# Making the normalised rows early, pairing the rows and summing in 32-column strips at the hand-over from the feed-forward block to the spectral block (backward pass, one core)

## Chip, cores, metric

One core of one Trainium2 chip. The metric is the device time of one execution in microseconds (us). The engines are TensorE (PE in the profile; PEld is its weight load), VectorE (DVE), ScalarE (ACT), GpSimd (POOL) and SyncE (SP).

A ratio below is the mean time of one kernel's fast runs over the mean of the kernel before's fast runs of the same rounds, with a 95% interval. It is therefore not quite the ratio of the medians that are quoted beside it.

## The reference

A block with two branches, forward and backward, in bf16. Cut to what matters:

```python
def _A_ref(x, w_r, w_i):                       # spectral branch
    X = rfft2(x.astype(float32)); X = X * (w_r + 1j * w_i)
    return irfft2(X, s=(S, D)).astype(bfloat16)
def _B_ref(x, w_gate, w_up, w_down):           # gated feed-forward
    g = x @ w_gate; u = x @ w_up
    return (g * u) @ w_down
mod = silu(c) @ w_mod                          # sa, ca, ga, sb, cb, gb: six rows of 576
h = layernorm(x) * (1 + ca) + sa
x1 = x + ga * _A_ref(h)
h = layernorm(x1) * (1 + cb) + sb
out = x1 + gb * _B_ref(h)
# returned: out and the gradients of x, w_r, w_i, w_gate, w_up, w_down, c, w_mod
```

S = 2048 rows, D = 576, F = 4608. The kernel holds the rows as 16 tiles of 128 rows; "a row" below is such a tile, 128 x 576, and j counts them. n is the normalised x1, y the output of the spectral branch, b the gradient that reaches the second layernorm's output, and gx the gradient of x1.

Three sums over all 2048 rows are wanted for the gradients of the modulation: the sum of b (for sb), of b * n (for cb) and of gx * y (for ga).

## The kernel before

The feed-forward backward is a loop of 18 steps (about 300 to 1186 us). Then comes the hand-over, to which the change belongs. For each row it

- finishes b with the last four products of the loop (`gh2_last`), whose result shrinks to bf16 in the first half of the row's fp32 accumulator. The freed second half (`acc_h`) then takes the row x1 that is loaded,
- normalises x1 on ScalarE, goes backward through the layernorm on VectorE and ScalarE, and stores gx,
- forms the three sums on TensorE, and
- begins the spectral backward (`fold`, then `stage_a`).

Remaining matmuls of the loop's weight gradients ("filler") are mixed in, so that TensorE has work while rows are prepared. Their results leave PSUM through VectorE (`gwd_halves`) or ScalarE (`gw_block`), and their banks come from the same ring as those of `gh2_last` and `stage_a`. Cut:

```python
def gh2_last(j):
    for h in range(2):
        b = sbk()                                          # next bank of the ring
        gh2_mms(NP - 1, j, h, bank[:, b, 0:288])
        tt(acc_b(j)[:, hs], acc[:, j, hs], bank[:, b, 0:288], ADD)      # VectorE

def diag_sums(a, b, j, b0, b1, c1, col):                   # sum of a*b on the diagonal of a^T b
    for m, (d0, n) in enumerate(CH):                       # chunks 128,128,128,128,64
        if col is not None:
            mm(bank[0:n, b1, col + m:col + m + 1], a[:, d0:d0 + n], ones[:, 0:1], ...)
        mm(..., a[:, d0:d0 + n], b[:, d0:d0 + n], ...)     # 128x128, its diagonal is used

def load_n(j):
    nx[j] = nx_r.next() if j < 2 else acc_h(j)
    sp.dma_start(nx[j][:], x1_d[:, j, :])                  # SyncE's queue

def row_front(j):
    n = nx[j]
    act(n[:], n[:], ACT.Identity, bias=nmr2[:, j:j + 1], scale=rstd2[:, j:j + 1])
    ...ln_bwd_a: gn = b*(1+cb), sum of gn, t2 = gn*n, sum of t2
def row_back(j):
    ...ln_bwd_b: gx from gn, n and the two sums; gx stored; fold(gx*(ga))
def row_sums(j):
    diag_sums(acc_b(j), nx[j], j, 2, 3, 0, 192)
    diag_sums(st_a[j][0], yl[j], j, 5, 3, 64, None)        # gx and y

for j in range(18):                                        # cut
    want = min(16, 2 + 5 * j // 4)
    while done < want: gh2_last(done); done += 1; ...fill.run(1.0)
    while loaded < min(done, j + 3): load_n(loaded); loaded += 1
    if j < 16: row_front(j); row_back(j)
    if fill.left() > 12.0 or j > 15: fill.run(1.0 if j < 16 else 2.0)
    if 2 <= j: row_sums(j - 2)
    if fill.left() > 12.0 or j > 15: fill.run(1.0)
    if 2 <= j: row_a(j - 2)                                # stage_a
```

After the loop, stage B of the spectral backward begins with the rest of the filler. A further filler follows, the forward's down projection ("the first y matmul").

Of the kernel before, what the change touches and what calls it, by code (L numbers as in the profile page):

```python
# [81 lines left out]
def build(ctx, tc, A_x, A_w_r, A_w_i, B_w_gate, B_w_up, B_w_down, c_in, w_mod, grad_out,  # L82
# [8 lines left out]
    def dram(name, shape, dt=BF):  # L91
        return nc.dram_tensor(name, list(shape), dt).ap()
# [5 lines left out]
    x1_d = dram("x1_d", [128, 16, D])  # L98
    gx1_d = dram("gx1_d", [128, 16, D])
# [109 lines left out]
    with tc.manual_schedule(engines={PE}):  # L209
# [756 lines left out]

        po.memset(gbacc[:], 0.0)
        for p in range(NP):
            gu_block(p)
            if p + 1 < NP:  # L970
                load_wgu(p + 1)
                load_wT(p + 1)
            load_wd(p)
            if p == NP - 1:
                break
            if p:
                for _, f in grads(p - 1, dbank):
                    f()
            else:
                for k in range(3):  # L980
                    transposes(k)
            for j in range(16):
                gh2_block(p, j)
# [4 lines left out]
        nx_r = Ring(span(ST, 2, 1152), [D])  # L988
        yl_r = Ring(span(ST + 2304, 2, 1152) + span(ST, 2, 1152), [D])
        F_r = Ring(span(ST + 4608, 4, 1152), [D])  # L990
        tg_r = Ring(span(ST + 9216, 3, 1152), [D])
        gx_r = Ring(span(ST + 12672, 3, 1152), [D])
        t2_r = Ring(span(ST + 16128, 4, 1152), [D])
        s_r = Ring([8704, 8736, 8768, 9952], [8], FP32)
        sring = [0, 1, 4, 6, 7]
# [25 lines left out]
        def diag_sums(a, b, j, b0, b1, c1, col):  # L1021

            for m, (d0, n) in enumerate(CH):
                if col is not None:
                    mm(bank[0:n, b1, col + m:col + m + 1], a[:, d0:d0 + n], ones[:, 0:1], j == 0 and m == 0, False, skip_group_check=True)
                if m < 4:
                    mm(bank[:, b0, 128 * m:128 * m + 128], a[:, d0:d0 + n], b[:, d0:d0 + n], j == 0 and m == 0, False, skip_group_check=True)
                else:
                    mm(bank[0:64, b1, c1:c1 + 64], a[:, 512:576], b[:, 512:576], False, False, skip_group_check=True)

        def column_sums(srcs, b, j, w):

            for h in range(2):
                for i, a in enumerate(srcs):
                    mm(bank[w * i:w * i + w, b + h, 0:288], ones[:, 0:w], a[:, 288 * h:288 * h + 288], j == 0, j == 15, skip_group_check=True)

# [5 lines left out]

        def load_n(j):

            nx[j] = nx_r.next() if j < 2 else acc_h(j)
            sp.dma_start(nx[j][:], x1_d[:, j, :])
# [53 lines left out]
        def row_front(j):  # L1100
            n = nx[j]
            act(n[:], n[:], ACT.Identity, bias=nmr2[:, j:j + 1], scale=rstd2[:, j:j + 1])
            gn, t2, s = tg_r.next(), t2_r.next(), s_r.next()
            ln_bwd_a(acc_b(j), n, mod[:, SCB, :], gn, None, t2, s)
            st_a[j] = (gn, t2, s)

        def row_back(j):
            gn, t2, s = st_a[j]
            gx, Fj = gx_r.next(), F_r.next()
            ln_bwd_b(nx[j], gn, t2, rstd2[:, j:j + 1], go[:, j, :], gx, s)  # L1110
            po.dma_start(gx1_d[:, j, :], gx[:])
            tt(gn[:], gx[:], mod[:, SGA, :], MUL)
            fold(Fj.unsqueeze(1), gn.unsqueeze(1), 1)
            st_a[j] = (gx, Fj)

        def row_sums(j):
            diag_sums(acc_b(j), nx[j], j, 2, 3, 0, 192)
            diag_sums(st_a[j][0], yl[j], j, 5, 3, 64, None)

        def row_a(j):  # L1120
            b = sbk()
            stage_a(st_a[j][1], b)
            evac_a(ac, b, j)
            if j % 2:
                b = sbk()
                for i in range(2):
                    stage_a_rem(st_a[j - 1 + i][1], b, i)
                evac_rem(ac, b, j - 1, 2)

        for j in range(2):  # L1130
            load_n(j)
            load1(yl, yl_r, y_d, j, sp)
        load_wdr(0, 9)
        done, loaded = 0, 2
        for j in range(18):
            want = min(16, 2 + 5 * j // 4)
# [5 lines left out]
            while loaded < min(done, j + 3):  # L1142
                load_n(loaded)
                loaded += 1
            if j < 16:
                row_front(j)
                row_back(j)
            if fill.left() > 12.0 or j > 15:
                fill.run(1.0 if j < 16 else 2.0)
            if 2 <= j < 18:  # L1150
                row_sums(j - 2)
            if fill.left() > 12.0 or j > 15:
                fill.run(1.0)
            if 2 <= j < 18:
                row_a(j - 2)
            if j < 14:
                load1(yl, yl_r, y_d, j + 2, sp)
# [4 lines left out]
            if j == 12:  # L1162
                load_wdr(9, 28)
                sp.dma_start(TI.rearrange("p a b c -> p (a b c)"), tabs["TI"][:, :])
                sp.dma_start(TBI.rearrange("p a b -> p (a b)"), tabs["TBI"][:, :])
            if j == 15:
                for t in W_r.t:
                    po.memset(t[:, :, :, DF:FP], 0.0)
                for u in range(2):
                    Ws[u] = W_r.next()  # L1170
                    load_W(Ws[u], u)
        sring = [4, 5]
# [14 lines left out]
        mk_r = Ring(span(ST + 16128, 2, 1152) + span(ST + 4608, 2, 1152), [D])  # L1187
# [9 lines left out]
        def diag_mask(b0, c1):  # L1197
            mk = mk_r.next()
            po.memset(mk[64:128, 512:576], 0.0)
            tt(mk[:, 0:512].rearrange("p (m d) -> p m d", m=4), bank[:, b0, :].rearrange("p (m d) -> p m d", m=4), ident.unsqueeze(1).to_broadcast([128, 4, 128]), MUL)  # L1200
            tt(mk[0:64, 512:576], bank[0:64, 3, c1:c1 + 64], ident[0:64, 0:64], MUL)
            return mk

        def col_mask(col):
            mk, cc = mk_r.next(), s_r.next()
            po.memset(mk[64:128, 512:576], 0.0)
            ve.tensor_copy(cc[:, 0:5], bank[:, 3, col:col + 5])
            for m, (d0, n) in enumerate(CH):
                ts(mk[0:n, d0:d0 + n], ident[0:n, 0:n], cc[0:n, m:m + 1], None, MUL)
            return mk  # L1210

        m_sga, m_scb, m_ssb, gbh = diag_mask(5, 64), diag_mask(2, 0), col_mask(192), mk_r.next()
        ve.tensor_copy(gbh[:], gbacc[:])

        def spread(rows, hi, lo):
            for h in range(2):
                for q0, src in ((0, hi), (64, lo)):
                    mm(bank[q0:q0 + 64, 6 + h, 0:288], ones[:, 0:64], src[:, 288 * h:288 * h + 288], True, True)
            ac.copy(halves(rows), bank[:, 6:8, 0:288])
# [55 lines left out]
        for s in range(9):  # L1275
# [3 lines left out]
            if s < 8:  # L1279
# [4 lines left out]
                if s == 0:  # L1284
                    spread(rows23, m_sga, m_ssb)
                fill.run(1.2)
                if s == 0:
                    spread(rows45, m_scb, gbh)
# [188 lines left out]
```

## Time and profile before

| | us |
|---|---|
| median of 15 runs | 1507.25 (1504.47 to 1509.69) |
| profiled execution | 1506.7 |
| loop, 350 to 1150 us: TensorE busy | 800.0 of 800 |
| hand-over, 1185.86 to 1285.40: TensorE busy | 87.4 of 99.5 |
| stage B up to the first y matmul | 9.3 |
| the rest | 212.0 |

The head of the page:

```profile
span 1506.7 us, 28428 instructions
...
PE 1467.3 (97%) x11221; PEld 981.1 (65%) x11244; DVE 779.9 (52%) x1734; ACT 548.5 (36%) x1048; POOL 345.8 (23%) x504
```

The table of stretches of the kernel before. Its columns are the stretch, its length, then busy time and instruction count per engine, the granted TensorE clock, the DMA share and GB/s. The second row is the hand-over, the third stage B.

```profile
core 0: us, PE busy (x) PEld busy (x) DVE busy (x) ACT busy (x) POOL busy (x), PEclk, DMA share, GB/s
350.00:1150.00 800.00, 800.00 (x6203) 562.09 (x6201) 340.63 (x620) 176.56 (x358) 164.00 (x226) 1.00 0.62 137
1185.86:1285.40 99.54, 87.41 (x873) 68.93 (x872) 72.13 (x208) 62.09 (x134) 26.13 (x41) 0.95 0.85 231
1285.40:1294.67 9.27, 9.27 (x83) 6.42 (x81) 2.19 (x3) 3.98 (x8) 0.33 (x3) 1.00 0.88 254
1294.67:1506.70 212.03, 200.46 (x1664) 144.47 (x1661) 150.28 (x341) 106.48 (x233) 54.81 (x86) 0.98 0.72 194
```

TensorE is full in the loop, where nothing is to be had, and loses time in the hand-over. The list of waits of the hand-over (who waited for whom, us in total, how often, the longest) says for what:

```profile
ACT arena L1102 <- DMA arena<-x_d: 14.0, 3, 6.3
DVE arena L1006 <- ACT arena L1102: 13.5, 5, 6.4
...
PE bank L943 <- ACT arena L889: 6.1, 2, 5.0
```

L1102 is the normalisation, and it waits for the load of x1. SyncE's queue in order of time shows the load (x_d) behind two transposing transfers, which hold the queue for 6.74 us together:

```profile
1222.57 6.74 SPq L830 DMA_TRANSPOSE arena<-arena  x2
1229.41 0.59 SPq L1046 DMA_DIRECT2D arena<-x_d  x1
1230.09 0.40 SPq L1050 DMA_DIRECT2D arena<-y_d  x1
```

The stop that follows can be traced through ScalarE, VectorE and TensorE in the timeline. The bracket is the idle time before an instruction, with what ended it.

```profile
1234.70 0.87 ACT L1102 ACTIVATE arena<-arena 128x576 bf16<-128x576 bf16 x1 [6.30 <-DMA arena<-x_d]
...
1235.60 0.46 DVE L1006 TENSOR_TENSOR arena<-arena 128x576 bf16<-128x576 bf16 x1 [6.43 <-ACT arena L1102]
...
1237.97 0.40 PE L943 MATMUL bank<-arena 128*128 128x288 bf16 x1 [4.95 <-ACT arena L889]
...
1238.16 0.44 PE L944 MATMUL bank<-arena 128*128 128x288 bf16 x1
...
1238.40 0.44 PE L945 MATMUL bank<-arena 128*128 128x288 bf16 x1
```

TensorE stood for 4.95 us. After that its 288-column matmuls start every 0.24 us instead of every 0.122 us. The Trainium skill says so of an array that has been idle for a while ("TensorE: Matmul & The Clock Gate", part 1). The stops of the hand-over add up to 12.1 us, and slow matmuls cost about 4 us more.

The sums of one row in TensorE's timeline take 1.07 us, from the start at 1208.51 to 1209.58:

```profile
1207.63 1.04 PE L888 MATMUL bank<-arena 128*128 128x256 bf16 x8
1208.51 0.17 PE L1025 MATMUL bank<-arena 128*128 128x1 bf16 x1
1208.53 0.22 PE L1027 MATMUL bank<-arena 128*128 128x128 bf16 x1
...
1209.43 0.22 PE L1029 MATMUL bank<-arena 128*64 128x64 bf16 x1
1209.58 1.05 PE L884 MATMUL bank<-arena 128*128 128x256 bf16 x8
```

### The profile page before, as it was taken

Reading aid. Unit: us, or ns where it says so; the run is one execution under the profiler, and the core shown is the slowest. Engines: PE = TensorE matmul, PEld = TensorE weight load, DVE = VectorE, ACT = ScalarE, POOL = GpSimd, SP = SyncE. Lnnn points to the kernel's source line nnn. Section 1 sums busy time; section 2 is a strip of 40 time slices with the busy share of each in tenths; the row PEclk is TensorE's granted clock in tenths of the full one; section 3 lists DMA queues with packets and bytes.
Section 4 is the critical chain, followed back from the end, with each engine's and each line's share of the span. In section 5 each row is a group of like instructions: output and inputs, shape, how many; then the busy total and the mean of one; then the engine's idle time right before and its main releaser. Section 6 shows DMA issues by size and latency. Waiting matters only on the chain.

```text
span 1506.7 us, 28428 instructions
## 1 busy us (share of the span) xinstructions
PE 1467.3 (97%) x11221; PEld 981.1 (65%) x11244; DVE 779.9 (52%) x1734; ACT 548.5 (36%) x1048; POOL 345.8 (23%) x504
## 2 busy tenths in 40 slices
PE   8999999999999999999999999999999988999998
PEld 5444444677667667667667668668668566776666
DVE  6533596543543443443453453453353776577766
ACT  6756675212221221221221221221221575333565
POOL 1344322203202202202202202202201113232211
PEclk9999999999999999999999999999999999999999
DMA  9656987958558548548548557557557469788873
GB/s 340 179 149 157 234 232 177 207 116 192 113 104 190 126 93 188 133 94 181 134 91 183 133 110 164 133 114 160 135 110 148 121 176 289 202 215 207 249 225 98
DMA packets 428762, 248.67 MB, mean 165 GB/s; under 512 B 319154, under 2 KB 403060, under 8 KB 428116
## 3 DMA queue, kind: packets, MB, share of 16 engines
q1 hardware_dynamic: 400418, 162.40, 48.6%
q0 software_dynamic: 27440, 83.65, 18.2%
q8 instruction: 88, 1.44, 0.4%
q10 hardware_dynamic: 770, 0.80, 0.2%
q14 instruction: 46, 0.38, 0.1%
HBM read 96.46 MB, written 74.20 MB: 113 GB/s over the span
## 4 chain that ended last, share of the span: by engine, by line
PE 84%; ACT 4%; DMA 4%; DVE 4%; issue 3%; POOL 1%; SPq 1%; DVEq 0%; POOLq 0%; ACTq 0%
PE bank L806 9%; PE bank L837 8%; PE bank L808 8%; PE bank L884 8%; PE bank L888 8%; PE bank L1082 6%; PE bank L943 5%; PE bank L946 4%; PE bank L945 4%; PE bank L944 4%; PE bank L370 3%; PE bank L801 3%; PE bank L374 3%; PE bank L904 2%; DMA arena<-in_w_mod_dram 1%
## 5 line engine op out<-in xcount | busy, mean ns | idle before, releaser
L957 DVE TENSOR_TENSOR arena<-arena,bank 128x576 f32<-128x576 f32 x256 | 193.1, 754 | 305.1 <-PE bank L946 305.1
L812 ACT CAST arena<-bank 128x512 bf16<-128x512 f32 x144 | 84.4, 586 | 384.6 <-PE bank L802 375.8
L943 PE MATMUL bank<-arena 128*128 128x288 bf16 x576 | 164.3, 285 | 6.3 <-ACT arena L889 6.1
L946 PE MATMUL bank<-arena 128*128 128x288 bf16 x576 | 164.9, 286 | 0.0
L945 PE MATMUL bank<-arena 128*128 128x288 bf16 x576 | 164.7, 286 | 0.0
L944 PE MATMUL bank<-arena 128*128 128x288 bf16 x576 | 164.4, 285 | 0.0
L884 PE MATMUL bank<-arena 128*128 128x256 bf16 x1152 | 149.5, 273 | 0.6 <-ACT arena L889 0.6
L888 PE MATMUL bank<-arena 128*128 128x256 bf16 x1152 | 149.8, 273 | 0.0
L1082 PE MATMUL bank<-arena 128*128 128x288 bf16 x1152 | 149.3, 288 | 0.2 <-ACT arena L1085 0.2
L806 PE MATMUL bank<-arena 128*128 128x512 bf16 x576 | 149.1, 381 | 0.0
L808 PE MATMUL bank<-arena 128*128 128x512 bf16 x576 | 147.8, 379 | 0.0
L1082 PEld LDWEIGHTS <-arena 128*128 128x128 bf16 x1152 | 112.0, 98 | 32.1 <-issue 3.5
L837 PE MATMUL bank<-arena 128*128 128x288 bf16 x1024 | 128.1, 286 | 0.0
L884 PEld LDWEIGHTS <-arena 128*128 128x128 bf16 x1152 | 110.7, 98 | 17.3 <-issue 4.5
L888 PEld LDWEIGHTS <-arena 128*128 128x128 bf16 x1152 | 112.4, 98 | 13.9 <-issue 0.2
L889 ACT CAST arena<-bank 128x256 bf16<-128x256 f32 x144 | 53.6, 372 | 185.4 <-PE bank L888 185.3
L837 PEld LDWEIGHTS <-arena 128*128 128x128 bf16 x1024 | 100.2, 98 | 28.2
L816 DVE TENSOR_TENSOR arena<-arena 128x512 bf16<-128x512 bf16 x144 | 61.3, 425 | 103.6 <-ACT arena L812 99.7
L734 POOL DMA_DIRECT2D arena<-ghh_d x36 | 20.1, 559 | 398.3 <-DVE arena L815 364.1
L806 PEld LDWEIGHTS <-arena 128*128 128x128 bf16 x576 | 50.5, 98 | 78.7 <-issue 31.5
L808 PEld LDWEIGHTS <-arena 128*128 128x128 bf16 x576 | 56.4, 98 | 68.0 <-issue 0.2
L813 ACT CAST arena<-bank 128x512 bf16<-128x512 f32 x144 | 84.8, 589 | 23.1 <-PE bank L808 23.1
(261 smaller groups left out, 2357.7 us busy)
## 6 DMA issues: line engine op xcount, KB each, us to landing
ghh_d<-arena POOLq DMA_DIRECT2D x72, 256.0 KB, 3.9
arena<-ghh_d POOLq DMA_DIRECT2D x36, 512.0 KB, 6.0
hh_d<-arena SPq DMA_DIRECT2D x36, 512.0 KB
arena<-hh_d SPq DMA_DIRECT2D x16, 1152.0 KB
out_dram<-arena POOLq DMA_DIRECT2D x67, 144.0 KB, 4.7
out_dram<-arena POOLq DMA_DIRECT2D x36, 256.0 KB, 5.1
arena<-in_B_w_down_dram POOLq DMA_DIRECT2D x18, 288.0 KB, 4.4
arena<-in_B_w_gate_dram POOLq DMA_DIRECT2D x18, 256.0 KB, 3.5
```

The costliest lines, as they stand in the source:

```text
L806: mm(bank[:, bg, :], w[:, m, fs], h2T[:, js, m, :], odd == 0 and m == 0, odd == 1 and m == 3)
L808: mm(bank[:, bu, :], w[:, 4 + k, fs], h2T[:, js, m, :], odd == 0 and k == 0, odd == 1 and k == 3)
L813: ac.copy(u[:], bank[:, bu, :])
L837: mm(bank[:, b0 + h, 0:288], sf[:, 0, fb, j, :], go[:, j, 288 * h:288 * h + 288], j == 0, j == 15)
L884: mm(bank[:, st["b"], 0:256], h2p[:, j, 128 * m:128 * m + 128], sf[:, 1 + w, :, j, :], j == 0, False)
L888: mm(bank[:, st["b"], 0:256], h2p[:, j, 128 * m:128 * m + 128], sf[:, 1 + w, :, j, :], False, j == 15)
L943: mm(o, xT[:, 1, 0, cs], wT[p][:, 0, 0, hs], True, False)
L944: mm(o, xT[:, 2, 0, cs], wT[p][:, 0, 1, hs], False, False)
L945: mm(o, xT[:, 1, 1, cs], wT[p][:, 1, 0, hs], False, False)
L946: mm(o, xT[:, 2, 1, cs], wT[p][:, 1, 1, hs], False, True)
L957: tt(dst, dst, src, ADD)
L1082: mm(bank[:, yb, 0:288], hl[:, fb % 18, 128 * (j % 2):128 * (j % 2) + 128], wdr[:, fb, 288 * h:288 * h + 288], fb == 0, fb == 35)
```

## The change

Its intent has three parts. First, make the normalised rows n in the loop, where ScalarE has time, and load them through GpSimd's queue instead of SyncE's. Second, do the layernorm backward on pairs of rows, with fewer and wider VectorE instructions and the scaling moved to ScalarE. Third, replace the diagonal products by column sums of b, b*n and gx*y: the products are made on VectorE and summed on TensorE by matmuls with ones in strips of 32 columns. With that the last products run one row further ahead, PSUM bank 3 joins the ring, gx is stored through SyncE's queue instead of GpSimd's, y is loaded in pairs of rows, and the weight rows of the later filler load in a different order. Cut to its core:

```diff
+        def keep_n(j):                                    # once a step, in the loop
+            t = prod_r.next().bitcast(BF)[:, 0:D]
+            d = t if j < 14 else nrow[:, j - 14, :]
+            po.dma_start(t, x1_d[:, j, :])
+            act(d, t, ACT.Identity, bias=nmr2[:, j:j + 1], scale=rstd2[:, j:j + 1])
+            if j < 14:
+                sp.dma_start(n_d[:, j, :], d)
...
-        sring = [0, 1, 4, 6, 7]
+        sring = [0, 1, 3, 4, 6, 7]
...
-        def diag_sums(a, b, j, b0, b1, c1, col):          # cut
+        def quarter_sums(a, b, q, start, stop):
+            for h in range(2):
+                r = slice(32 * (q + h), 32 * (q + h) + 32)
+                mm(bank[r, b, 0:288], ones[:, 0:32], a[:, 288 * h:288 * h + 288], start, stop, ...)
...
         def load_n(j):
-            nx[j] = nx_r.next() if j < 2 else acc_h(j)
-            sp.dma_start(nx[j][:], x1_d[:, j, :])
+            if j < 14:
+                po.dma_start(acc_h(j), n_d[:, j, :])
...
+        def front(i):                                     # a pair of rows
+            tt(gn[:], b_pair(i), opc, MUL)
+            tt(q[:], b_pair(i), n, MUL)
+            tt(t2[:], q[:], opc, MUL)
+            for k in range(2):
+                act(gn[:, k, :], gn[:, k, :], ACT.Copy, scale=rstd2[...], accum_out=s[:, k, 0:1])
+                act(t2[:, k, :], t2[:, k, :], ACT.Copy, scale=nrs2[...], accum_out=s[:, k, 1:2])
+        def back(i):
+            ...gx, its store (SyncE), gx*(ga), fold
+            tt(t2[:], gx[:], yl[i][:], MUL)
+        def sums_1(j):
+            quarter_sums(acc_b(j), 2, 0, j == 0, j == 15)
+            quarter_sums(st_a[j // 2][2][:, j % 2, :], 2, 2, j == 0, j == 15)
+        def sums_2(i):
+            for k in range(2):
+                quarter_sums(st_a[i][1][:, k, :], 5, 2 * k, i == 0, i == 7)
...
-        for j in range(18):
-            want = min(16, 2 + 5 * j // 4)
+        for j in range(19):
+            want = min(16, 3 + 5 * j // 4)
...
-            while loaded < min(done, j + 3):
+            while loaded < min(done, j + 6):
```

More of the change, by code (lines that the diff above doesn't have):

```diff
@@ L98, in build @@
     x1_d = dram("x1_d", [128, 16, D])
+    n_d = dram("n_d", [128, 16, D])
     gx1_d = dram("gx1_d", [128, 16, D])
@@ L965, in gh2_last @@
                 tt(acc_b(j)[:, hs], acc[:, j, hs], bank[:, b, 0:288], ADD)
+        nrow = mod[:, SSA:SSB + 1:SSB - SSA, :]
+        def keep_n(j):
[5 more added lines that the diff above has]
+                sp.dma_start(n_d[:, j, :], d)
         po.memset(gbacc[:], 0.0)
@@ L976, in build @@
             if p:
-                for _, f in grads(p - 1, dbank):
+                for i, (_, f) in enumerate(grads(p - 1, dbank)):
                     f()
+                    if i == 7 and p > 1:
+                        keep_n(p - 2)
+                        if p == NP - 2:
+                            keep_n(p - 1)
             else:
@@ L987, in build @@
         pl = NP - 1
-        nx_r = Ring(span(ST, 2, 1152), [D])
-        yl_r = Ring(span(ST + 2304, 2, 1152) + span(ST, 2, 1152), [D])
-        F_r = Ring(span(ST + 4608, 4, 1152), [D])
-        tg_r = Ring(span(ST + 9216, 3, 1152), [D])
-        gx_r = Ring(span(ST + 12672, 3, 1152), [D])
-        t2_r = Ring(span(ST + 16128, 4, 1152), [D])
+        yl_r = Ring(span(ST, 2, 2304), [2, D])
+        gn_r = Ring(span(ST + 4608, 3, 2304), [2, D])
+        t2_r = Ring(span(ST + 11520, 3, 2304), [2, D])
+        q_r = Ring(span(ST + 18432, 2, 2304), [2, D])
+        gx_r = Ring(span(ST + 23040, 2, 2304), [2, D])
         s_r = Ring([8704, 8736, 8768, 9952], [8], FP32)
-        sring = [0, 1, 4, 6, 7]
+        nrs2 = small[:, 82:98]
+        sring = [0, 1, 3, 4, 6, 7]
         fill = Fill()
@@ L1019, in build @@
         CH = [(0, 128), (128, 128), (256, 128), (384, 128), (512, 64)]
-        def diag_sums(a, b, j, b0, b1, c1, col):
-            for m, (d0, n) in enumerate(CH):
-                if col is not None:
-                    mm(bank[0:n, b1, col + m:col + m + 1], a[:, d0:d0 + n], ones[:, 0:1], j == 0 and m == 0, False, skip_group_check=True)
-                if m < 4:
-                    mm(bank[:, b0, 128 * m:128 * m + 128], a[:, d0:d0 + n], b[:, d0:d0 + n], j == 0 and m == 0, False, skip_group_check=True)
-                else:
-                    mm(bank[0:64, b1, c1:c1 + 64], a[:, 512:576], b[:, 512:576], False, False, skip_group_check=True)
         def column_sums(srcs, b, j, w):
@@ L1035, in column_sums @@
                     mm(bank[w * i:w * i + w, b + h, 0:288], ones[:, 0:w], a[:, 288 * h:288 * h + 288], j == 0, j == 15, skip_group_check=True)
+        def quarter_sums(a, b, q, start, stop):
+            for h in range(2):
+                r = slice(32 * (q + h), 32 * (q + h) + 32)
+                mm(bank[r, b, 0:288], ones[:, 0:32], a[:, 288 * h:288 * h + 288], start, stop, skip_group_check=True)
         nx, yl, Ws = {}, {}, {}
@@ L1041, in acc_h, with n_pair, b_pair, load_yl @@
             return acc[:, j, 288:576].bitcast(BF)
+        def n_pair(i):
+            return acc[:, 2 * i:2 * i + 2, 288:576].bitcast(BF) if i < 7 else nrow
+        def b_pair(i):
+            return acc[:, 2 * i:2 * i + 2, 0:288].bitcast(BF)
         def load_n(j):
-            nx[j] = nx_r.next() if j < 2 else acc_h(j)
-            sp.dma_start(nx[j][:], x1_d[:, j, :])
+            if j < 14:
+                po.dma_start(acc_h(j), n_d[:, j, :])
+        def load_yl(i):
+            yl[i] = yl_r.next()
+            sp.dma_start(yl[i][:], y_d[:, 2 * i:2 * i + 2, :])
         def load1(d, ring, src, j, eng):
@@ L1098, in build @@
         st_a = {}
-        def row_front(j):
-            n = nx[j]
-            act(n[:], n[:], ACT.Identity, bias=nmr2[:, j:j + 1], scale=rstd2[:, j:j + 1])
-            gn, t2, s = tg_r.next(), t2_r.next(), s_r.next()
-            ln_bwd_a(acc_b(j), n, mod[:, SCB, :], gn, None, t2, s)
-            st_a[j] = (gn, t2, s)
-        def row_back(j):
-            gn, t2, s = st_a[j]
-            gx, Fj = gx_r.next(), F_r.next()
-            ln_bwd_b(nx[j], gn, t2, rstd2[:, j:j + 1], go[:, j, :], gx, s)
-            po.dma_start(gx1_d[:, j, :], gx[:])
-            tt(gn[:], gx[:], mod[:, SGA, :], MUL)
-            fold(Fj.unsqueeze(1), gn.unsqueeze(1), 1)
-            st_a[j] = (gx, Fj)
@@ L1116, in row_sums, with two @@
-        def row_sums(j):
-            diag_sums(acc_b(j), nx[j], j, 2, 3, 0, 192)
-            diag_sums(st_a[j][0], yl[j], j, 5, 3, 64, None)
+        def two(row):
+            return row.unsqueeze(1).to_broadcast([128, 2, D])
+        def front(i):
+            gn, t2, q, s = gn_r.next(), t2_r.next(), q_r.next(), s_r.next().rearrange("p (k v) -> p k v", k=2)
+            n, opc = n_pair(i), two(mod[:, SCB, :])
+            tt(gn[:], b_pair(i), opc, MUL)
+            tt(q[:], b_pair(i), n, MUL)
+            tt(t2[:], q[:], opc, MUL)
+            for k in range(2):
+                j = 2 * i + k
+                act(gn[:, k, :], gn[:, k, :], ACT.Copy, scale=rstd2[:, j:j + 1], accum_out=s[:, k, 0:1])
+                act(t2[:, k, :], t2[:, k, :], ACT.Copy, scale=nrs2[:, j:j + 1], accum_out=s[:, k, 1:2])
+            st_a[i] = (gn, t2, q, s)
@@ new lines, in back @@
+        def back(i):
+            gn, t2, q, s = st_a[i]
+            gx, n = gx_r.next(), n_pair(i)
+            ts(s[:, :, 0], s[:, :, 0], -1.0 / D, None, MUL)
+            for k in range(2):
+                act(t2[:, k, :], n[:, k, :], ACT.Identity, bias=s[:, k, 0:1], scale=s[:, k, 1:2])
+            tt(gn[:], gn[:], t2[:], ADD)
+            tt(gx[:], gn[:], go[:, 2 * i:2 * i + 2, :], ADD)
+            sp.dma_start(gx1_d[:, 2 * i:2 * i + 2, :], gx[:])
+            tt(t2[:], gx[:], two(mod[:, SGA, :]), MUL)
+            fold(gn, t2, 2)
+            tt(t2[:], gx[:], yl[i][:], MUL)
@@ L1120, in row_a @@
+        def sums_1(j):
+            quarter_sums(acc_b(j), 2, 0, j == 0, j == 15)
+            quarter_sums(st_a[j // 2][2][:, j % 2, :], 2, 2, j == 0, j == 15)
+        def sums_2(i):
+            for k in range(2):
+                quarter_sums(st_a[i][1][:, k, :], 5, 2 * k, i == 0, i == 7)
         def row_a(j):
+            Fj = st_a[j // 2][0]
             b = sbk()
-            stage_a(st_a[j][1], b)
+            stage_a(Fj[:, j % 2, :], b)
             evac_a(ac, b, j)
@@ L1126, in row_a @@
                 for i in range(2):
-                    stage_a_rem(st_a[j - 1 + i][1], b, i)
+                    stage_a_rem(Fj[:, i, :], b, i)
                 evac_rem(ac, b, j - 1, 2)
-        for j in range(2):
-            load_n(j)
-            load1(yl, yl_r, y_d, j, sp)
-        load_wdr(0, 9)
-        done, loaded = 0, 2
-        for j in range(18):
-            want = min(16, 2 + 5 * j // 4)
+        ts(nrs2, rstd2, -1.0 / D, None, MUL)
+        for i in range(2):
+            load_yl(i)
+        load_wdr(6, 9)
+        done, loaded = 0, 0
+        for j in range(19):
+            want = min(16, 3 + 5 * j // 4)
             while done < want:
@@ L1141, in build @@
                     fill.run(1.0)
-            while loaded < min(done, j + 3):
+            while loaded < min(done, j + 6):
                 load_n(loaded)
                 loaded += 1
-            if j < 16:
-                row_front(j)
-                row_back(j)
+            if j % 2 == 0 and j < 16:
+                front(j // 2)
+                back(j // 2)
+                if 2 <= j < 14:
+                    load_yl(j // 2 + 1)
             if fill.left() > 12.0 or j > 15:
                 fill.run(1.0 if j < 16 else 2.0)
-            if 2 <= j < 18:
-                row_sums(j - 2)
+            if 1 <= j < 17:
+                sums_1(j - 1)
             if fill.left() > 12.0 or j > 15:
                 fill.run(1.0)
-            if 2 <= j < 18:
-                row_a(j - 2)
-            if j < 14:
-                load1(yl, yl_r, y_d, j + 2, sp)
+            if 3 <= j:
+                if j % 2 == 0:
+                    sums_2(j // 2 - 2)
+                row_a(j - 3)
             if j == 4:
@@ L1162, in build @@
             if j == 12:
-                load_wdr(9, 28)
+                load_wdr(9, 19)
+                load_wdr(19, 28)
                 sp.dma_start(TI.rearrange("p a b c -> p (a b c)"), tabs["TI"][:, :])
@@ L1171, in build @@
                     load_W(Ws[u], u)
+            if j == 16:
+                load_wdr(0, 6)
         sring = [4, 5]
@@ L1184, in build @@
         Y_t, SD_t = V(RC + U, [2, 2, FP]), V(RC + 2 * U, [4, FP])
-        mk_r = Ring(span(ST + 16128, 2, 1152) + span(ST + 4608, 2, 1152), [D])
+        sums = V(ST + 16128, [2, 288])
+        gbh, even_odd = V(ST + 5376, [D]), V(ST + 4864, [2, 64])
         rows23, rows45 = mod[:, SSB, :], mod[:, SCB, :]
@@ L1195, in halves @@
             return t.rearrange("p (h d) -> p h d", h=2)
-        def diag_mask(b0, c1):
-            mk = mk_r.next()
-            po.memset(mk[64:128, 512:576], 0.0)
-            tt(mk[:, 0:512].rearrange("p (m d) -> p m d", m=4), bank[:, b0, :].rearrange("p (m d) -> p m d", m=4), ident.unsqueeze(1).to_broadcast([128, 4, 128]), MUL)
-            tt(mk[0:64, 512:576], bank[0:64, 3, c1:c1 + 64], ident[0:64, 0:64], MUL)
-            return mk
-        def col_mask(col):
-            mk, cc = mk_r.next(), s_r.next()
-            po.memset(mk[64:128, 512:576], 0.0)
-            ve.tensor_copy(cc[:, 0:5], bank[:, 3, col:col + 5])
-            for m, (d0, n) in enumerate(CH):
-                ts(mk[0:n, d0:d0 + n], ident[0:n, 0:n], cc[0:n, m:m + 1], None, MUL)
-            return mk
-        m_sga, m_scb, m_ssb, gbh = diag_mask(5, 64), diag_mask(2, 0), col_mask(192), mk_r.next()
-        ve.tensor_copy(gbh[:], gbacc[:])
+        ve.tensor_copy(gbh[:], gbacc[:])
+        for i, b in enumerate((2, 5)):
+            ve.tensor_copy(sums[:, i, :], bank[:, b, 0:288])
+        ve.memset(even_odd[:], 0.0)
+        for q in range(4):
+            ve.memset(even_odd[32 * q:32 * q + 32, q % 2, :], 1.0 / 32)
         def spread(rows, hi, lo):
             for h in range(2):
+                hs = slice(288 * h, 288 * h + 288)
                 for q0, src in ((0, hi), (64, lo)):
-                    mm(bank[q0:q0 + 64, 6 + h, 0:288], ones[:, 0:64], src[:, 288 * h:288 * h + 288], True, True)
+                    o = bank[q0:q0 + 64, 6 + h, 0:288]
+                    if src == "gb":
+                        mm(o, ones[:, 0:64], gbh[:, hs], True, True)
+                    elif src == "ga":
+                        mm(o, even_odd[:, h, :], sums[:, 1, :], True, True)
+                    else:
+                        r = slice(src + 32 * h, src + 32 * h + 1)
+                        mm(o, ones[r, 0:64], sums[r, 0, :], True, True)
             ac.copy(halves(rows), bank[:, 6:8, 0:288])
@@ L1284, in build @@
                 if s == 0:
-                    spread(rows23, m_sga, m_ssb)
+                    spread(rows23, "ga", 0)
                 fill.run(1.2)
                 if s == 0:
-                    spread(rows45, m_scb, gbh)
+                    spread(rows45, 64, "gb")
             if s >= 4:
```

## The prediction

> **What bounds the kernel now.** TensorE: 1467 of 1507 us busy (the page's first part), and the table of stretches shows 800.0 of 800 us in the feed-forward loop (350 to 1150 us) at full clock. The loop cannot be helped by this change. Its target is the hand-over after it, about 1186 to 1285 us, where TensorE is busy only 86.9 of 99 us. In the timeline of that stretch TensorE stops for 1.1, 1.1, 0.4, 0.6, 4.95 and 3.9 us, 12.1 us together. The list of waits and the SyncE queue show why: loads of the residual rows (x1) sit in SyncE's queue behind transposing transfers (6.7 and 7.1 us in the queue), ScalarE's normalisation waits 6.3 and 5.8 us for them, VectorE 6.4 and 4.8 us for ScalarE, TensorE for both. After the two long stops matmuls of 288 columns take 0.24 instead of 0.122 us for some microseconds, as the Trainium skill ("TensorE: Matmul & The Clock Gate", part 1) says of an idle array; I count 4 us lost. So stops and slow clock are worth 16 us.
>
> **What the change does.**
> - Normalised rows are made in the loop and stored; the hand-over loads them through GpSimd's queue, up to six rows ahead. That takes 16 ScalarE operations of 0.87 us off the hand-over and the load off the chain behind the transposes. In the loop ScalarE is busy 177 of 800 us and evacuation has several banks in hand: I expect no cost there (0 to 2 us).
> - Diagonal products (15 matmuls a row, 1.07 us by the timeline, 17 us for 16 rows) become column sums in 32-column strips: four matmuls a row and four a pair. Two-strip matmuls in this trace start within 10 ns of each other, with about 0.1 us lost entering and leaving the strip mode (the skill, "TensorEngine Tiling (Array Packing)", Key Properties, says a mode switch drains). Estimate: 0.33 us a group, 24 groups, 8 us. TensorE saves about 9 us; if strips did not overlap four-fold, 3 to 5.
> - VectorE: pairs instead of rows, fewer instructions, but two new products. By issue intervals (0.37 us for 576 columns, hence about 0.67 for 1152; 0.22 for a fold half), 3.4 us a row before and 3.5 after: neutral, about 62 us of a 78 us hand-over. ScalarE falls from about 4.7 to 3.8 us a row.
> - New risks: y is now consumed by VectorE in order, and its loads still stand behind the transposes with one pair (about 9 us) of slack; a third of the weight rows loads late, when DMA is already at its limit (share about 1.0 from 1250 to 1300 us).
>
> **Sum.** TensorE work -8, stops and cold clock 16 down to about 5 (-11), loop and late loads +1: about -18 us, all on the critical path. Predicted 1488 us, range 1478 to 1499. Over 2% faster needs 30 us, more than the stage can lose: 0.06; within 2%: 0.91; over 2% slower: 0.03.
>
> **What would show it.** Hand-over about 80 us instead of 99; TensorE idle there below 6 us, no stop over 3 us, no 0.24 us matmuls; ScalarE no longer waiting for x1 loads; strip matmuls starting in fours; loop still 800 of 800 us; the time after stage B unchanged (within 3 us).
>
> **What would make it wrong.** The y product stalling VectorE behind the transposes, so that a 5 us stop comes back; the load in the loop holding ScalarE long enough to exhaust the four banks (1 us sixteen times would eat the gain); late weight rows or h tiles stopping TensorE before the first y matmuls; the strips running one after the other.

## More of the kernel before

TensorE's program order is written by hand. The order of every other engine is chosen when the kernel is built, from estimated times, and is then fixed.

## The result and the profile after

| | before | after |
|---|---|---|
| median | 1507.25 (15 runs) | 1496.0 (10 runs, 1489.96 to 1502.41) |
| ratio | | 0.9921 [0.9905, 0.9936] |
| profiled execution | 1506.7 | 1494.7 |
| hand-over | 99.5 | 88.7 |
| stage B up to the first y matmul | 9.3 | 8.4 |
| the rest | 212.0 | 212.5 |

```profile
span 1494.7 us, 28176 instructions
...
PE 1456.3 (97%) x11077; PEld 967.6 (65%) x11100; DVE 777.8 (52%) x1668; ACT 547.3 (37%) x1048; POOL 353.9 (24%) x515
```

The same stretches of the changed kernel:

```profile
core 0: us, PE busy (x) PEld busy (x) DVE busy (x) ACT busy (x) POOL busy (x), PEclk, DMA share, GB/s
350.00:1150.00 800.00, 800.00 (x6204) 562.08 (x6203) 339.32 (x619) 185.10 (x373) 172.40 (x242) 1.00 0.64 143
1185.05:1273.74 88.69, 81.53 (x769) 60.16 (x768) 70.48 (x141) 53.82 (x122) 25.53 (x36) 0.96 0.81 236
1273.74:1282.17 8.43, 6.06 (x43) 3.20 (x40) 2.19 (x3) 3.58 (x6) 0.91 (x3) 1.00 1.14 321
1282.17:1494.70 212.53, 199.35 (x1664) 143.83 (x1661) 150.33 (x341) 105.87 (x232) 54.03 (x85) 0.99 0.73 199
```

The loop is still full and the rest is unchanged. Nearly the whole gain of 12.0 us in this pair of executions lies between the start of the hand-over and the first y matmul, 108.8 us before and 97.1 after. TensorE now also stops in stage B, for 2.4 us (8.43 minus 6.06). The filler that covered it before has been used up by then: 40 of stage B's 83 matmuls there were filler, and the change has 43 in all.

The loop's work for n has no cost there. ScalarE waits 169 us in all for the x1 rows, 10.6 us each, and TensorE does not notice:

```profile
ACT arena L975 <- DMA arena<-x_d: 169.4, 16, 12.8
```

The strips are as hoped. In TensorE's timeline four of them (x4) fit between two filler blocks:

```profile
1193.87 1.14 PE L863 MATMUL bank<-arena 128*128 128x288 bf16 x8
1194.94 0.31 PE L1047 MATMUL bank<-arena 128*32 128x288 bf16 x4
1195.18 1.15 PE L863 MATMUL bank<-arena 128*128 128x288 bf16 x8
```

The first block's eight matmuls need 8 x 0.122 us and so have entered by 1194.85, and the next block begins at 1195.18. A group of four therefore takes 0.33 us, and there are 24 groups: 7.9 us instead of 16 x 1.07 = 17.1.

The stops did not go away. From the waits of the hand-over:

```profile
DVE arena L1129 <- DMA arena<-n_d: 3.9, 1, 3.9
PE bank L446 <- DVE arena L871: 3.8, 1, 3.8
...
PE bank L885 <- DVE arena L871: 2.0, 1, 2.0
```

Here is the longest, followed through the timeline. L1064 is the load of a row n on GpSimd's queue, L1129 is b*n of the pair (here the sixth pair, rows 10 and 11), L871 is the second of two reads that free a bank of the filler, and L446 is the part of `stage_a` that waits for that bank.

```profile
1227.05 0.54 POOL L1064 DMA_DIRECT2D arena<-n_d  x1 [1.85 <-DVE arena L966]
```

```profile
1229.41 0.21 DVE L1140 TENSOR_SCALAR arena<-arena 128x2 f32<-128x2 f32 x1
1233.52 0.76 DVE L1129 TENSOR_TENSOR arena<-arena 128x1152 bf16<-128x1152 bf16 x1 [3.90 <-DMA arena<-n_d]
...
1240.37 0.75 DVE L1148 TENSOR_TENSOR arena<-arena 128x1152 bf16<-128x1152 bf16 x1
...
1241.11 0.45 DVE L870 TENSOR_TENSOR arena<-bank,arena 128x288 bf16<-128x288 f32 x1
1241.47 0.45 DVE L871 TENSOR_TENSOR arena<-bank,arena 128x288 f32<-128x288 f32 x1
```

```profile
1241.98 0.22 PE L446 MATMUL bank<-arena 128*32 128x128 bf16 x1 [3.81 <-DVE arena L871]
...
1242.52 0.45 PE L946 MATMUL bank<-arena 128*128 128x288 bf16 x1
1242.76 0.45 PE L947 MATMUL bank<-arena 128*128 128x288 bf16 x1
```

The load shown is the twelfth, so that of row 11; it is the last one that this product needs. (The semaphores in the trace say the same: the product waits for the two that the loads of rows 10 and 11 count up. The load issued next, at 1229.12, is for row 12.) It was issued at 1227.05, after a wait of 1.85 us for VectorE's last addition of the row (L966), because only that addition frees the half accumulator into which the load goes. VectorE reached L1129 at 1229.6, 2.6 us after the issue, and stood until 1233.52, 6.5 us after it. Its queue is executed in order ("ACT/DVE are strict FIFO", the Trainium skill, "TensorE: Matmul & The Clock Gate", part 1). So the bank's release came 4 us late too, although its matmuls had long ended, and TensorE stood for 3.81 us and then ran slowly.

I split the stretch from the first product of the hand-over to the first y matmul into stops (the brackets in TensorE's timeline), slow clock (start-to-start times above those at full speed, added up by hand) and the rest, which is work with its mode switches:

| one profiled execution each | stretch | stops | slow clock | rest |
|---|---|---|---|---|
| before | 108.8 | 12.1 | about 4 | 92.6 |
| after | 97.1 | 9.5 | about 3.5 | 84.1 |

Work fell by 8.5 us. Stops and slow clock fell only from 16 to 13 us. (The granted clock of the profile, read as for the next table, gives 4.5 and 3.4 us of slow clock.)

### The profile page after: what moved, and what is told of

The parts are those of the page before. It is cut to its first block, busy times and chain, and to the rows that moved or that the text cites. A ratio compares the mean times of both kernels' runs of the same rounds, so it can differ in the third digit from the quotient of the medians.

```text
span 1494.7 us, 28176 instructions
## 1 busy us (share of the span) xinstructions
PE 1456.3 (97%) x11077; PEld 967.6 (65%) x11100; DVE 777.8 (52%) x1668; ACT 547.3 (37%) x1048; POOL 353.9 (24%) x515
## 4 chain that ended last, share of the span: by engine, by line
PE 78%; issue 6%; DVE 5%; DMA 5%; ACT 4%; POOL 1%; SPq 0%; DVEq 0%; ACTq 0%; POOLq 0%
PE bank L807 8%; PE bank L838 8%; PE bank L885 8%; PE bank L889 8%; PE bank L809 8%; PE bank L1104 5%; PE bank L944 5%; PE bank L946 4%; PE bank L947 4%; PE bank L945 4%; PE bank L802 2%; PE bank L371 2%; PE bank L375 2%; PE bank L905 2%; DMA arena<-in_w_mod_dram 2%
## 5 line engine op out<-in xcount | busy, mean ns | idle before, releaser
L813 ACT CAST arena<-bank 128x512 bf16<-128x512 f32 x144 | 84.3, 585 | 385.0 <-PE bank L803 376.8
```

## The experiments

Twelve runs were made, in three sets of four, each set on one chip with the kernel before among them. "Stops" include stage B. The table gives the outcome, and the expectations follow.

| run | median | ratio [95%] | stretch | stops | slow | rest |
|---|---|---|---|---|---|---|
| n alone | 1497.61 | 0.9939 [0.9926, 0.9953] | 99.9 | 5.7 | 1.7 | 92.5 |
| diagonal products back (faulty) | 1507.23 | 1.0005 [0.9992, 1.0019] | 109.3 | 13.8 | 3.0 | 92.5 |
| diagonal products back (mended) | 1500.83 | 0.9967 [0.9953, 0.9980] | 103.1 | 10.4 | 0.0 | 92.6 |
| n resident | 1492.46 | 0.9905 [0.9890, 0.9920] | 93.6 | 7.7 | 1.7 | 84.2 |
| rows ahead | 1489.4 | 0.9895 [0.9878, 0.9912] | 90.7 | 6.9 | 0.0 | 83.9 |
| rows not pairs | 1492.88 | 0.9915 [0.9901, 0.9930] | 94.6 | 8.3 | 1.7 | 84.6 |
| rows ahead, filler kept | 1489.8 | 0.9889 [0.9874, 0.9904] | 91.4 | 6.9 | 0.0 | 84.5 |
| rows not pairs, ahead, filler kept | 1491.25 | 0.9903 [0.9888, 0.9918] | 92.6 | 7.2 | 0.0 | 85.4 |
| the change, again | 1494.76 | 0.9926 [0.9914, 0.9938] | 94.0 | 8.0 | 1.7 | 84.3 |
| without the y product | 1496.15 | 0.9946 [0.9920, 0.9972] | 96.6 | 8.2 | 4.1 | 84.3 |
| y product twice | 1501.14 | 0.9962 [0.9949, 0.9975] | 100.3 | 12.6 | 3.3 | 84.4 |
| rows ahead, n resident | 1489.61 | 0.9886 [0.9872, 0.9901] | 91.6 | 7.2 | 0.0 | 84.4 |

Here "slow" is half the time that TensorE worked while its granted clock, as the profile records it, was one half. The last column says that TensorE's work is about 84 us (83.9 to 85.4) wherever strips are used and about 92.5 where they are not, whatever else is done.

One limit holds for all of them. An edit also changes the order that the build chooses for VectorE, ScalarE and the queues, so no edit is quite alone.

### n alone (e1)

```diff
@@ kernel before @@
+        (keep_n in the loop, as in the change)
-            sp.dma_start(nx[j][:], x1_d[:, j, :])
+            if j < 14:
+                po.dma_start(nx[j][:], n_d[:, j, :])      # rows 14, 15 are resident
-            act(n[:], n[:], ACT.Identity, bias=nmr2[:, j:j + 1], scale=rstd2[:, j:j + 1])
-            while loaded < min(done, j + 3):
+            while loaded < min(done, j + 6):
```

> The kernel before with one part of the change alone: normalised rows made in the loop and loaded through GpSimd's queue up to six rows ahead; rows one by one and diagonal products as before. If the loads of x1 behind the transposes made the stops (theory A), the 12.1 us of TensorE stops in the hand-over fall below 7 us, the slow clock after them mostly goes, and the time falls by 6 to 10 us, to about 1498. If the gain of the change comes from the strips alone (rival B), this run is within 2 us of before and has about 12 us of stops.

Measured: 1497.61 us, 0.61% or about 9 us faster, with stops of 5.7 us and 1.7 us of slow clock. That is what theory A expected, and this part alone brings most of the gain. TensorE's work (92.5 us) is that of before. One rival is not separated: the run also takes 16 normalisations of 0.87 us off ScalarE, whose copies TensorE had waited for, and no run moves the loads alone. The trace of the kernel before speaks for the loads: ScalarE itself stood 6.30 us for one. VectorE still waits for rows n here, 5.2 us in all, 2.4 us at most.

### Diagonal products back (e2, f4)

```diff
@@ changed kernel @@
-            quarter_sums(acc_b(j), 2, 0, j == 0, j == 15)
-            quarter_sums(st_a[j // 2][2][:, j % 2, :], 2, 2, j == 0, j == 15)
+            diag_sums(acc_b(j), n_pair(j // 2)[:, j % 2, :], j, 2, 3, 0, 192)
-                quarter_sums(st_a[i][1][:, k, :], 5, 2 * k, i == 0, i == 7)
+                diag_sums(st_a[i][2][:, k, :], yl[i][:, k, :], 2 * i + k, 5, 3, 64, None)
-            tt(t2[:], gx[:], yl[i][:], MUL)               # and t2 = gn*n without q
-        sring = [0, 1, 3, 4, 6, 7]
+        sring = [0, 1, 4, 6, 7]
@@ f4 only @@
-            if j == 16:
+            if j == 18:
                 load_wdr(0, 6)
```

> The changed kernel with the diagonal products put back in place of the strip sums (and without the two VectorE products that the strips need). Theory C, TensorE work counts one to one: 17.1 us of sums instead of 7.9, so about 9 us slower than the change, near 1505. Rival D, VectorE is what holds the hand-over: it loses two products of 0.67 us a pair, 10.7 us in all, stops shrink below 3 us, and the run is within 3 us of the change, near 1497.

The first version was faulty. The late weight rows were loaded into buffers that the last pair's sums had still to read, so two outputs were wrong. TensorE also waited 3.5 us for that load in front of those sums. Its time tells nothing about the question, and it was mended:

> The run with the diagonal products put back, mended: the late weight rows are loaded after the last sums, so results are right. The same time within 2 us, near 1507: TensorE has 8 us more to do than in the change, and the stops do not shrink.

Measured: 1500.83 us, so the expectation of 1507 (taken from the faulty run) was missed by 6. Against the change, which ran in other rounds (0.9921 and 0.9926), the strips are worth 0.4 to 0.5%, 6 to 7 us. TensorE has about 8.5 us more work without them. Its stops and slow clock are 10.4 us, against 13.0 and 9.7 in two executions of the change. So most of the work counts (theory C). A small part may be given back as stops, but the two executions of the change differ by as much as that part. Rival D, that VectorE's two products set the time here, is refuted: without them the kernel is slower. (The edit also takes bank 3 out of the ring again, gives y two more pair buffers and moves the sums of gx and y one step earlier.)

### No row loads in the hand-over (e3)

```diff
@@ changed kernel @@
-            return acc[:, 2 * i:2 * i + 2, 288:576].bitcast(BF) if i < 7 else nrow
+            return nrow
-            if j < 14:
-                po.dma_start(acc_h(j), n_d[:, j, :])
+            pass
```

> The changed kernel with no load of normalised rows in the hand-over: every pair uses the one pair that is resident (wrong results on purpose, for what depends on them). Theory E, the remaining stops (7.2 us and 3.5 us of slow clock) come from VectorE waiting in order for those loads: the 3.8 us stop goes, and the time falls by 4 to 7 us from the change, to about 1490. Rival F, they come from evacuations of the filler's banks queued on VectorE behind 0.75 us pair products: stops stay at 5 us or more, time within 2 us of the change.

Measured: 1492.46 us, ratio 0.9905. That is 2 to 3 us faster than the change by the ratios, less than the 4 to 7 expected; the intervals overlap. The 3.8 us stop is gone (the longest is 1.8 us), and so is the slow clock in the hand-over; in this execution 1.7 us of it fell into stage B. Stops of 7.7 us remain. (The wrong rows enter the outputs so weakly that the comparison with the reference passed. It is still not a valid kernel.)

### The last products three rows further ahead (e4)

```diff
@@ changed kernel @@
-            want = min(16, 3 + 5 * j // 4)
+            want = min(16, 6 + 5 * j // 4)
-            while loaded < min(done, j + 6):
+            while loaded < min(done, j + 9):
```

> The changed kernel with the last products (which free the buffers for the loads) run three rows further ahead, and loads up to nine rows ahead; results unchanged. Theory E: loads are issued some 10 us earlier, so most of their latency is hidden, 3 to 5 us faster than the change, near 1492. Rival F: the filler's evacuations are still behind the pair products: within 2 us of the change.

Measured: 1489.4 us, ratio 0.9895, 4 to 5 us faster than the change by the ratios (5 to 7 by the medians), the upper end of what was expected or more; results are right. Its table of stretches (hand-over, stage B):

```profile
1185.18:1267.50 82.32, 77.75 (x770) 58.55 (x769) 71.33 (x141) 53.14 (x122) 25.86 (x36) 1.00 0.90 252
1267.50:1275.92 8.42, 6.05 (x42) 3.20 (x40) 2.19 (x3) 3.58 (x6) 0.94 (x3) 1.00 1.10 343
```

Its hand-over is 82.3 us, at full clock. In TensorE's timeline its first stops, which are the longest but one of 1.6 us, wait for ScalarE's copies out of PSUM, not for a chain behind a load:

```profile
1210.45 0.28 PE L944 MATMUL bank<-arena 128*128 128x288 bf16 x1 [1.22 <-ACT arena L890]
...
1232.75 1.14 PE L863 MATMUL bank<-arena 128*128 128x288 bf16 x8 [1.28 <-ACT arena L890]
```

No wait of VectorE for a row n is left in its list of waits.

### Rows instead of pairs (f1)

```diff
@@ changed kernel @@
-            if j % 2 == 0 and j < 16:
-                front(j // 2)
-                back(j // 2)
+            if j < 16:
+                front(j)                                  # the same operations on one row,
+                back(j)                                   # in the same buffers
```

> The changed kernel with its pair operations undone: the same operations, buffers and loads, but on one row of 576 columns at a time, front and back of a row every step. Theory P, the pairs cost stops (in the run with n alone, row by row, stops and slow clock were 7.4 us; in the change 13.4): stops and slow clock fall to 7 to 9 us and the time by 4 to 6 us from the change, to about 1491. Theory Q, the strips leave TensorE 8 us less to do while VectorE has the same work, so the stops are what VectorE's load makes them, whatever the grouping: no gain, stops 12 to 15 us, time within 2 us of the change or slower (a row costs VectorE about 0.2 us more in instruction overhead, 3 us in all).

Measured: 1492.88 us, ratio 0.9915 against 0.9921 and 0.9926. The stops and slow clock, 10.0 us, lie between what P and Q expected, and the intervals overlap. It is inconclusive. What can be said is that the pairs do not pay by themselves here, although VectorE is busy 76.1 us instead of 70.5 in the hand-over without them.

### Rows ahead with filler kept, and both (f2, f3)

```diff
@@ e4, and f1 with e4 @@
-                fill.run(1.0 if j < 16 else 2.0)
+                fill.run(1.0)
```

> The changed kernel with the last products three rows further ahead (as in the run before, 1489.4 us) and with half of the filler of the last three steps kept for stage B, where the change left TensorE 2.4 us of stops. If the missing filler makes those stops, they go and the time falls by about 2 us from 1489.4, to 1487.5; if not, the time stays at 1489.

Measured: 1489.8 us against 1489.4. The stops in stage B fell from 2.4 to 0.8 us as expected, and those of the hand-over rose from 4.5 to 6.1. The filler can be spent in one place or the other, and the time does not move. The expected 2 us were not there.

> Row by row, strips, last products three rows ahead, filler kept. Theory P: it adds to the run with pairs ahead, about 1485. Theory Q: VectorE has 3 us more to do than with pairs, so no faster than the pairs with the same order, 1488 to 1491.

Measured: 1491.25 us. Rows instead of pairs add nothing once the products run ahead. This is about what Q expected, and P's 1485 is refuted.

### The change again, with less and with more VectorE work, and ahead without loads (g1 to g4)

> The changed kernel unaltered, on the same chip and in the same rounds as the next three: near 1496, ratio about 0.992; stops and slow clock between 10 and 16 us.

Measured: 1494.76 us, ratio 0.9926, in agreement with the first result. This execution took 1490.1 us in the profile, 4.6 us less than the first, with the same kernel. The same load (row 11) and its consumer:

```profile
1226.38 0.54 POOL L1064 DMA_DIRECT2D arena<-n_d  x1 [1.85 <-DVE arena L966]
```

```profile
1228.73 0.21 DVE L1140 TENSOR_SCALAR arena<-arena 128x2 f32<-128x2 f32 x1
1230.78 0.76 DVE L1129 TENSOR_TENSOR arena<-arena 128x1152 bf16<-128x1152 bf16 x1 [1.83 <-PE bank L947]
```

```profile
1239.23 0.22 PE L446 MATMUL bank<-arena 128*32 128x128 bf16 x1 [1.74 <-DVE arena L871]
...
1240.26 0.45 PE L945 MATMUL bank<-arena 128*128 128x288 bf16 x1
```

Here VectorE goes on 4.40 us after the load's issue, instead of 6.47 us. It stands 1.83 us instead of 3.90, and TensorE's stop is 1.74 us instead of 3.81. All three differences are 2.07 us. (The bracket names a matmul as releaser, but this product reads no bank. It waits for the semaphores of the loads of rows 10 and 11.) This is the clearest evidence for theory E: along this chain nothing differs but the load's duration. What made it longer is not shown. The two executions differ elsewhere too: after the same stop at the start of the hand-over, 2.00 us in the first and 1.99 us here, the granted clock fell to one half for 3.4 us in the first and stayed full here, which is worth 1.7 us. Loads and clock together may be why the change's times scatter by 12 us where those of before scatter by 5. The two kernels without row loads scatter by 1.4 and 0.9 us in four runs each, which fits but does not prove it.

```diff
@@ g2 @@
-            tt(t2[:], gx[:], yl[i][:], MUL)
@@ g3 @@
             tt(t2[:], gx[:], yl[i][:], MUL)
+            tt(t2[:], gx[:], yl[i][:], MUL)
```

> The changed kernel without the product of gx and y on VectorE (8 operations of 0.67 us, 5.4 us in all; wrong on purpose in the two outputs that need it). Theory F, VectorE's queue is what holds TensorE where it still stops: 3 to 5 us faster than the unaltered run. Theory E, the row loads alone hold it: within 1.5 us.

> The changed kernel with that product made twice (results unchanged), 5.4 us more for VectorE. Theory F: 3 to 5 us slower than the unaltered run. Theory E: within 1.5 us.

Taking 5.4 us of VectorE work away gained nothing: stops of 8.2 us against 8.0, and more slow clock, 4.1 us against 1.7. The ratio 0.9946 has a wide interval, with one run at 1507.6, and the two outputs that need the product were wrong. Adding 5.4 us cost 0.36%, about 5 us, and the stops grew from 8.0 to 12.6 us:

```profile
1222.75 0.27 PE L446 MATMUL bank<-arena 128*32 128x128 bf16 x1 [3.75 <-ACT arena L890]
...
1249.43 0.38 PE L443 MATMUL bank<-arena 128*128 128x128 bf16 x4 [3.29 <-DVE arena L871]
```

Neither E nor F had this pair of results. VectorE has no slack for more in this stretch, but what remains is not bought back by giving it less. Its share of the hand-over is 70.5 of 85.6 us busy, and the order of its queue was changed by both edits.

> Last products three rows further ahead and no row loads at all in the hand-over (resident rows, wrong on purpose). If running ahead gained because it hides the row loads (theory E), taking them away adds nothing: within 2 us of 1489.5. If it gained by something else, for example by giving VectorE's row work an earlier start, the gains add: 1486 or less.

Measured: 1489.61 us, ratio 0.9886, against 0.9895 and 0.9889 for the two kernels ahead with loads. This is what theory E expected: once the last products run ahead, the row loads cost nothing that these runs can tell, so running ahead hides them. That this is all it does is not shown. Where no rows are loaded, running ahead still takes 2.9 us off (1492.46 to 1489.61; ratios 0.9905 and 0.9886, whose intervals overlap, and the slow clock in stage B of the first has a part in it).

The kernel with the last products three rows further ahead is right in its results and beats both kernels: 1489.4 us against 1496.0 and 1507.25.

## Why the prediction was right or wrong

The time was predicted as 1488 with a range of 1478 to 1499, and measured as 1496.0. The direction, the place and the class (within 2%) were right. The gain was 11 us, not 18 to 19. Point by point:

- **What bounds the kernel: right.** The loop stayed at 800.0 of 800 us, and the gain lies in the hand-over. That the x1 loads behind the transposes caused the two long stops is read from the trace, and n alone agrees: it takes 9 us off without touching TensorE's work (it takes the normalisations off ScalarE too).
- **TensorE's work, -8 us: right.** The strips run four at a time, 0.33 us a group as estimated, 7.9 us instead of 17.1. The rest column falls by 8.5 us in the profiled pair. Putting the diagonal products back adds about 8.5 us of work and 6 to 7 us of time.
- **"stops and cold clock 16 down to about 5 (-11)": the term that was mis-sized.** They went from 16 to 13 us in the profiled execution, and to 9.7 in another. The step behind it was "loads them through GpSimd's queue, up to six rows ahead". The code does say six, but a load cannot start before the last product of its own row has freed the half accumulator it goes into, and those products run only three rows ahead at the start (five later, by the formula). In the order that VectorE was given, the load of row 11 was issued 2.6 us before it was wanted, and took longer. VectorE waits for it in order, now directly instead of behind ScalarE, and TensorE waits for a bank that VectorE frees later. A difference in the load's duration comes out one to one in TensorE's stop (6.47 us from issue to use and 3.81 us of stop in one execution, 4.40 and 1.74 in another). Three rows more of lead remove the wait and gain 4 to 5 us, and without any row loads that kernel gains no more.
- **The clock.** I expected no matmuls at 0.24 us, and there were some after stops of 3.81, 2.0 and 1.74 us.
- **Stage B.** I expected the time after stage B to be unchanged, and it was (212.0 and 212.5). I did not see that the longer loop would use the filler up and open 2.4 us of stops in stage B. Keeping filler for it moved the stops without gain.
- **The loop, 0 to 2 us: right** (0). ScalarE waits there 10.6 us for each row and nothing depends on it.
- **VectorE neutral: right** in sum (72.1 to 70.5 us in the hand-over). **ScalarE from 4.7 to 3.8 us a row**, 14 us in all, was too much: 62.1 to 53.8 us, since stage lengths and filler copies count too.
- **The risks.** The y product never held VectorE in the changed kernel: no wait of VectorE for y is in its lists of waits (among the variants, rows not pairs has one, of 1.3 us). The late weight rows stopped nothing; the first y matmul comes 8.4 us after stage B begins, earlier than before. The named risks did not occur, and the one that did was not named.

What stays open: what each of the remaining 7 us of stops in the best version depends on (ScalarE's copies, the order of VectorE's queue), and whether pairs are worth anything. The parts do not add up either: 9 us for n alone and 6 to 7 us for the strips are more than the 11 to 12 us of the whole, and stops and slow clock are 7.4 us with n alone against 13.0 and 9.7 in the change. Whether the pairs or TensorE's shorter work give these 4 us back was not settled.

## What to carry to other kernels

How far ahead a load ran was set here by what freed its buffer, not by the number in the prefetch loop: look in the trace for what the issuing queue waits for just before the load. When a wait is removed from one engine in a chain of in-order queues, check which engine now meets the same latency, because the stop can come back one engine further on. Matmul work that is really removed from TensorE counted for most of its length here (6 to 7 of about 8.5 us), even in a stretch that also has stops.

## What the Trainium skill lacked or had wrong

- "TensorE: Matmul & The Clock Gate" (part 1 and the closing table) puts the return to the slow clock after an idle window of about 3.4 us and advises against gaps over about 3 us. Here the granted clock also fell to one half after stops of 2.00, 1.74 and 1.68 us (two executions of the change, and rows not pairs), and it stayed full after 1.99 us (the change, again), 2.20 us (rows not pairs, ahead, filler kept) and 2.97 us (without the y product). So the length of a stop alone did not tell. Each fall in these hand-overs lasted 3.4 or 6.8 us.
- "DMA: Bandwidth & Descriptors" (the fit for the GpSimd path, about 2.0 us + bytes / 436 GB/s) gives an estimate of 2.3 us for a row of 147,456 bytes. The loads of the hand-over whose landing the trace times took 2.6 us in the median, close to it, but the load that decided the stop had 6.5 and 4.4 us from issue to use in two executions of one kernel, with the DMA share at 0.93 and 1.09 meanwhile and transposing transfers just before it in both. The page's fit has no term for other traffic. What made the difference of 2.1 us is not shown.
- "TensorEngine Tiling (Array Packing)" (Key Properties) says that changing the tiling mode drains TensorE, without a figure. Here a group of four strips of 288 columns took 0.33 us where 0.12 us is the streaming time, so entering and leaving cost about 0.2 us together.
- No page that I read says what in-order queues do to PSUM banks shared by several users: a 3.9 us wait of VectorE for a load delayed the release of an unrelated bank and stopped TensorE for 3.8 us.
